# Stacking a short row chunk into 128 partitions with masked tables, and splitting more units of a fused Fourier and gated feed-forward kernel

## The chip, the cores and the metric

One NeuronCore of a Trainium2 chip runs the whole program. The metric is the device time of one execution in microseconds (us); medians are over the fast runs (granted TensorE clock 0.996 to 1.000). The engines are PE (TensorE, matmul), DVE (VectorE), ACT (ScalarE), POOL (GpSimd) and SP (which issues DMAs here).

## The reference

```
def reference(x, w_gate, w_val, w_out):          # x: 8 x 3008 x 256
    X = fft(fft(x, axis=1), axis=2).real         # Fourier mixing over rows and channels
    X = X.reshape(24064, 256)
    g = X @ w_gate                               # 256 -> 1536
    v = X @ w_val
    return (silu(g) * v) @ w_out                 # 1536 -> 256
```

## The kernel before

The row transform uses the symmetries of the Fourier sum. Each batch of 3008 rows is folded on POOL into cosine and sine coefficient rows: a chunk A of 128 rows and a short chunk C of 61 rows. Chunk C of two batches shares a 128-partition tile: the even batch has partitions 0 to 63, the odd one 64 to 127. PE multiplies the coefficients (weights) with tables `Tab` (moving side). A batch has two parts, each in two halves `eo`, each half with a `v` and a `g` product (`q`). The code is shortened:

```
def blocks(b, q):
    p0 = 64 * (b % 2)
    return [(0, slice(0, P), *coef_a(b)),                                 # chunk A: 128 rows
            (1, slice(p0, p0 + 64) if b else slice(0, P), *coef_c(b))]    # chunk C: 64 rows
...
for j, (ch, r, CE, BB) in enumerate(blk):
    for eo in eos:
        for kind in range(2):
            if part == 0:   # 189 or 188 columns, one block of columns for each kind
                cols = slice(0, GH + 1) if kind == 0 else slice(GH + 1, NCE)
                l, r_ = CE[r, q, eo, kind, 0:P], tab[:, eo, cols]
            else:           # 376 columns, both kinds added into the same ones
                l, r_ = BB[r, q, eo, kind, 0:P], tab[:, (eo + kind) % 2, NOO:NTAB]
            nc.tensor.matmul(ps[eo][:, cols], l, r_, ...)
if part == 0 and 1 in eos:
    row0(b, q, ps[1])       # weights of ONE column, result added to row 0 of ps[1]
# after each half: ACT copies v from PSUM (od), DVE adds and subtracts g and od into Pt, Qt
```

The transform of a batch is a job put between two "units" of the feed-forward part. A unit is one block of 128 hidden channels for one tile of up to 512 columns; there are 24 tiles of 12 units. A column pair (row k and row -k) shares the products with `Pt` and `Qt`. An unsplit unit takes 6 matmuls; a split one takes 5 and reconstructs the second value by an instruction on DVE and a multiplication on POOL:

```
SPLIT     = (0, 2, 3, 5, 6, 8, 9, 11)             # tiles 3 to 20
SPLIT_END = (0, 1, 2, 3, 5, 6, 7, 8, 9, 11)       # tiles 21, 22
def split(u):
    return 3 <= u[0] < nT - 1 and u[1] in (SPLIT if u[0] < t_end else SPLIT_END)

# part_a: g = Wp.Pt + Wq.Qt ; v = Wp.Pt
#   split:   ACT  sp = silu(g) ; DVE es = bc * w0 + v
#   unsplit: v += Wq.Qt ; ACT sg = silu(g) ; DVE hp = sg * v
# part_b (one unit later): g += Wm.Qt
#   split:   v += Wq.Qt ; DVE vv = 2 es - v ; ACT sgv = silu(g) ; POOL hm = sgv * vv ; DVE hp = sp * v
#   unsplit: v += Wm.Qt ; ACT sg = silu(g) ; DVE hm = sg * v
```

Between these, 8 output matmuls (`o<-Wo,hp` and `o<-Wo,hm`, 256 columns) of the tile before are put into each unit. The kernel uses eight banks of PSUM (the memory that matmuls write): three for `g`, three for `v`, two for the output.

Of the kernel before, what the change touches and what calls it, by code (L numbers as in the profile page):

```python
# [31 lines left out]
def kernel(  # L32
# [25 lines left out]
    t0 = [sum(wide[:t]) for t in range(nT)]  # L58


    NCE = 2 * GH + 1
    NOO = NCE + GH + 1
    NTAB = NOO + G
# [9 lines left out]

    const = ctx.enter_context(tc.tile_pool(name="const", bufs=1))
    cp = ctx.enter_context(tc.tile_pool(name="coef", bufs=2))
    pqp = ctx.enter_context(tc.tile_pool(name="pq", bufs=5))
    odp = ctx.enter_context(tc.tile_pool(name="od", bufs=2))
    psG = ctx.enter_context(tc.tile_pool(name="psG", bufs=3, space=bass.MemoryType.PSUM))
# [18 lines left out]
    sgn = const.tile([P, 1], F32, name="sgn")  # L97
    XA = const.tile([P, 8, 2, D], F32, name="XA")
    XC = const.tile([P, 8, 2, D], F32, name="XC")
    SDf = const.tile([P, 2, 4, D], F32, name="SDf")  # L100
    EOf = const.tile([P, 2, 4, P + 1], F32, name="EOf")
    Af = const.tile([P, 2, 2, P + 1], F32, name="Af")

# [42 lines left out]

    def fold_steps(eng, X, CE, BB, q, r):
        tt = eng.tensor_tensor
        F = SDf[r, q]
        E, O = EOf[r, 0], EOf[r, 1]  # L150
        up, down = X[r, 0:4, q], X[r, 7:3:-1, 1 - q]

        def cross():
            tt(F[:, :, 1:D], up[:, :, 1:D], down[:, :, D - 1:0:-1], op=Alu.add)
            tt(E[:, :, P:P + 1], up[:, :, 0:1], down[:, :, 0:1], op=Alu.add)

        def even():
            tt(E[:, :, 0:P], F[:, :, P:0:-1], F[:, :, P:D], op=Alu.add)

        def odd():  # L160
            tt(O[:, :, 0:P], F[:, :, P:0:-1], F[:, :, P:D], op=Alu.subtract)

        def ab():
            tt(Af[r], EOf[r, :, 0:2, :], EOf[r, :, 2:4, :], op=Alu.add)

        def ce():
            tt(CE[r, q, :, 0, :], Af[r, :, 0, :], Af[r, :, 1, :], op=Alu.add)
            tt(CE[r, q, :, 1, :], Af[r, :, 0, :], Af[r, :, 1, :], op=Alu.subtract)

        def bb():  # L170
            quarter_rows(tt, E, O, BB[r, q])

        return [cross, even, odd, ab, ce, bb]
# [3 lines left out]
        tt(B_[:, 1], O[:, 0:2, 0:P], O[:, 2:4, 0:P], op=Alu.subtract)  # L177
        tt(B_[:, 1, :, 0:1], E[:, 3::-3, P:P + 1], E[:, 1:3, P:P + 1], op=Alu.subtract)

    coefA, coefC = {}, {}  # L180

    def coef_a(b):
        if b not in coefA:
# [1 line left out]
                        cp.tile([P, 2, 2, 2, P], BF16, name="BBa"))  # L185
        return coefA[b]

    def coef_c(b):
        p = b if b < 2 else 1 + b // 2
        if p not in coefC:  # L190
            coefC[p] = (cp.tile([P, 2, 2, 2, P + 1], BF16, name="CEc"),
                        cp.tile([P, 2, 2, 2, P], BF16, name="BBc"))
        return coefC[p]



# [125 lines left out]
    def weigh(lo, hi):  # L322
        vts(Tab[:, 1, 1, :, lo:hi], Tab[:, 1, 1, :, lo:hi], scalar1=wC, scalar2=None, op0=Alu.mult)
# [8 lines left out]
            nc.gpsimd.dma_start(out=dst, in_=src.rearrange("(no p) f -> p no f", p=P)[:, :, fc * T:(fc + 1) * T])  # L332

    CEa, BBa = coef_a(0)
    CEc, BBc = coef_c(0)


    ti = [tp.tile([P, 2, NCE], I32, name=f"t1{ch}") for ch in range(2)]
# [63 lines left out]

    def heads(eng, ev, od, CE):

        eng.tensor_tensor(CE[:, :, 0, 0, P:P + 1], ev, od, op=Alu.add)
        eng.tensor_tensor(CE[:, :, 0, 1, P:P + 1], ev, od, op=Alu.subtract)

    acc = [[None, None], [None, None]]

# [128 lines left out]
    pl, ql = pq_tiles(nT - 1)  # L538
    last = (pl[:, w_last:w_last + B], ql[:, w_last:w_last + B])

    def blocks(b, q):

        p0 = 64 * (b % 2)
        return [(0, slice(0, P), *coef_a(b)), (1, slice(p0, p0 + 64) if b else slice(0, P), *coef_c(b))]

    def row0(b, q, ps):
        for ch, r, CE, BB in blocks(b, q):
            for kind, cols in ((0, slice(0, GH + 1)), (1, slice(GH + 1, NCE))):
                nc.tensor.matmul(ps[0:1, cols], CE[r, q, 0, kind, P:P + 1], Tab[r, ch, q, 0, cols],  # L549
                                 start=False, stop=True, skip_group_check=True)  # L550

    def transform(b, part, eos, given=None):
        n = NCE if part == 0 else G
        ev, ods = {}, {}
        for q, pool, nm in ((0, psV, "v"), (1, psG, "g")):
            if given:
                ps = {eo: given[eo][q] for eo in eos}
                blk = []
            else:
                ps = {eo: pool.tile([P, T], F32, name=nm) for eo in eos}  # L560
                blk = blocks(b, q)
            for j, (ch, r, CE, BB) in enumerate(blk):
                tab = Tab[r, ch, q]
                for eo in eos:
                    for kind in range(2):
                        if part == 0:
                            cols = slice(0, GH + 1) if kind == 0 else slice(GH + 1, NCE)
                            l, r_ = CE[r, q, eo, kind, 0:P], tab[:, eo, cols]
                        else:
                            cols = slice(0, G)  # L570
                            l = BB[r, q, eo, kind, 0:P]
                            r_ = tab[:, (eo + kind) % 2, NOO:NTAB]
                        nc.tensor.matmul(ps[eo][:, cols], l, r_, start=(j == 0 and kind == 0),  # L573
                                         stop=(j == len(blk) - 1 and kind == 1), skip_group_check=True)
            if part == 0 and 1 in eos and not given:

                row0(b, q, ps[1])
            for eo in eos:
                if q == 0:
                    ods[eo] = odp.tile([P, NCE], F32, name="od")  # L580
                    nc.scalar.copy(ods[eo][:, 0:n], ps[eo][:, 0:n])
                else:
                    ev[eo] = ps[eo]

        def put(eo, dst, s0, w, minus):
            nc.vector.tensor_tensor(dst, ev[eo][:, s0:s0 + w], ods[eo][:, s0:s0 + w],  # L586
                                    op=Alu.subtract if minus else Alu.add)

        if part == 0:
            runs = [(0, GH, 1, 0), (GH, GH, 0, 1), (G, GH, GH + 1, 0), (G + GH, GH, GH + 1, 1)]  # L590
        else:
            runs = [(2 * G, G, 0, 0), (3 * G, G, 0, 1)]
        todo = []
        for eo in eos:
            for c0, n_, s0, minus in runs:
                for t, off, src, w in pieces(b * H + c0, n_):
                    todo.append((t, eo, off, s0 + src, w, minus))
        for t, eo, off, s0, w, minus in sorted(todo, key=lambda v: v[0:2]):
            put(eo, pq_tiles(t)[eo][:, off:off + w], s0, w, minus)
        if part == 0:  # L600
            for eo in eos:
                put(eo, last[eo][:, b:b + 1], 0, 1, 0)
# [98 lines left out]
    state = {}  # L701
    owork = None

    SPLIT = (0, 2, 3, 5, 6, 8, 9, 11)
    SPLIT_END = (0, 1, 2, 3, 5, 6, 7, 8, 9, 11)
    t_end = tile_of((B - 1) * H) + 1

    bc = {}

    def split(u):  # L710

        return 3 <= u[0] < nT - 1 and u[1] in (SPLIT if u[0] < t_end else SPLIT_END)

    def part_a(u):
        t, f = u
# [31 lines left out]
    def part_b(u):  # L747
# [4 lines left out]
        fs = slice(f * P, (f + 1) * P)  # L752
        nc.tensor.matmul(g[:, :w], Wm[:, 0, fs], Qt[:, :w], start=False, stop=True, skip_group_check=True)  # L753
        if kept:
            nc.tensor.matmul(v[:, :w], Wq[:, 1, fs], Qt[:, :w], start=False, stop=True, skip_group_check=True)  # L755
            sp, es = kept
            vm = vvp.tile([P, T], F32, name="vv")
            nc.vector.scalar_tensor_tensor(vm[:, w - 1::-1], es[:, :w], 2.0, v[:, :w],  # L758
                                           op0=Alu.mult, op1=Alu.subtract)
            sm = sgv.tile([P, T], F32, name="sgv")  # L760
            nc.scalar.activation(sm[:, w - 1::-1], g[:, :w], AF.Silu)  # L761
            nc.gpsimd.tensor_tensor(hts[t][1][:, f, :w], sm[:, :w], vm[:, :w], op=Alu.mult)  # L762
            nc.vector.tensor_tensor(hts[t][0][:, f, :w], sp[:, :w], v[:, :w], op=Alu.mult)  # L763
            return
        nc.tensor.matmul(v[:, :w], Wm[:, 1, fs], Qt[:, :w], start=False, stop=True, skip_group_check=True)  # L765
        sg = sgp.tile([P, T], F32, name="sg")
# [21 lines left out]
        lo += 1  # L788
    queue = {}
    act_at = {}  # L790

    def run_loads(n):
        for _, fn in loads[:n]:
# [3 lines left out]
    def fold_step(what, i, unit):  # L797
# [4 lines left out]
        if j == 0:  # L802
            if kind == "A":
                queue[what] = fold_steps(nc.gpsimd, XA, *coef_a(b), q, slice(0, P))
            else:
                queue[what] = fold_steps(nc.gpsimd, XC, *coef_c(b), q, slice(64 if b == 1 else 0, P))
        queue[what].pop(0)()
        if q == 1 and j == 0:
            act_at.setdefault(max(unit + 2, 11), []).append(what)

    def load_next(what):
        kind, b = what
# [22 lines left out]
    def weight_unit(fc, gv):  # L835
        return [lambda k=k: weights(fc, gv, k) for k in range(2)]

    raO = SDf.rearrange("p k a d -> p (k a d)")[:, 0:4 * G].rearrange("p (c q n) -> p c q n", c=2, q=2)

    def angles_o(ch):  # L840
        return [lambda: angles(rrO[:, ch], kfO, ch, rrO[:, ch].bitcast(I32)),
# [5 lines left out]
    def sine_o(ch):  # L847
# [2 lines left out]
    before = {0: angles_o(0), 1: weight_unit(1, 0), 2: weight_unit(1, 1), 3: angles_o(1) + cosine_o(0),  # L850
              4: weight_unit(2, 0) + cosine_o(1), 5: weight_unit(2, 1), 7: sine_o(0), 8: sine_o(1),
              9: [lambda: weigh(NOO, NTAB), lambda: value_rows((1, 2))]}
    loads = []

    prev = None
    owork = None
    for i, u in enumerate(units):
        t, f = u
        if f == 0 and split((t, SPLIT[0])):
            ps = psG.tile([P, T], F32, name="g")  # L860
            w = width(t)
            nc.tensor.matmul(ps[:, :w], sel, pq_tiles(t)[1][:, :w], start=True, stop=True)  # L862
            bc.pop(t - 2, None)
            bc[t] = bcp.tile([P, T], F32, name="bc")
            nc.scalar.copy(bc[t][:, :w], ps[:, :w])
        for fn in before.pop(i, ()):
            fn()
# [14 lines left out]
            fold_step(what, j, i)  # L882
        for what in act_at.pop(i, ()):
            load_next(what)
        if i in job_at:
            whole_part(*job_at[i])
        prev = u
# [35 lines left out]
```

## Time and profile before

| reading | value |
|---|---|
| time, median (range) of 3 runs | 673.16 us (672.6 to 673.18) |
| PE / DVE / ACT / POOL busy | 98 / 82 / 65 / 63% of 670.8 us |
| chain that ended last | PE 94% |
| split units | 164 of 288 |
| length of a middle tile: no transform / with a part 0 / with a part 1 | 24.51 / 27.76 / 27.89 us |

A tile's length is the distance between the starts of its first `g` matmul and of the next tile's, read from the timeline. The head of the program is the part up to the first unit, mostly input DMAs.

The first lines of the profile of the kernel before (engine, busy us, share, instructions; PEld are PE's weight loads; then the chain of waits, by engine):

```profile
PE 656.5 (98%) x4269; PEld 411.6 (61%) x4336; DVE 549.4 (82%) x957; ACT 433.5 (65%) x764; POOL 423.8 (63%) x455
...
PE 94%; DVE 2%; DMA 2%; issue 1%; POOL 1%; ACT 0%; DVEq 0%; ACTq 0%; POOLq 0%
```

PE's 98% alone would prove little. The Trainium skill says so too ("Perfetto Trace Analysis", Identifying the Most-Contended Engine: matmul busy time is a bad measure, because matmuls are pipelined), and this case agrees: its profiles read 98, 97 and 98% for kernels of 671, 651 and 634 us. What counts is the distance between starts. In the timeline a 512-column matmul recorded as 0.38 us is followed by the next after 0.216 us. Apart from single steps of 0.43 us (a matmul whose record is missing), PE has no holes in units.

DVE must be read in the same way. The timeline of DVE in tile 22 of the kernel before, which already had 10 split units (start us, duration us, instruction):

```profile
628.75 0.74 DVE L735 SCALAR_TENSOR_TENSOR es<-bc,w,v 128x512 f32<-128x512 f32 x1
629.50 0.69 DVE L758 SCALAR_TENSOR_TENSOR vv<-es,v 128x512 f32<-128x512 f32 x1
630.11 0.68 DVE L763 TENSOR_TENSOR hp<-sp,v 128x512 bf16<-128x512 f32 x1
630.70 0.74 DVE L735 SCALAR_TENSOR_TENSOR es<-bc,w,v 128x512 f32<-128x512 f32 x1
```

The three durations add up to 2.11 us, yet the next round starts after 1.95 us: two of the three records run about 0.08 us into the next one. The 1.95 us are also PE's period (5 x 0.216 + 8 x 0.109), and two other rounds of this kernel are shorter (1.85 and 1.86 us). So DVE is led by PE here, although it looks full; e8 and e9 test it.

The timeline of PE in a part 0 of the kernel before (x2 merges two matmuls):

```profile
383.94 0.33 PE L573 MATMUL v<-Tab,CEa 128*128 128x189 bf16 x2
384.21 0.34 PE L573 MATMUL v<-Tab,CEc 64*128 64x189 bf16 x2
384.48 0.34 PE L573 MATMUL g<-Tab,CEa 128*128 128x189 bf16 x2
384.75 0.33 PE L573 MATMUL g<-Tab,CEc 64*128 64x189 bf16 x2
385.11 0.33 PE L573 MATMUL v<-Tab,CEa 128*128 128x189 bf16 x2
385.36 0.34 PE L573 MATMUL v<-Tab,CEc 64*128 64x189 bf16 x2
385.63 0.33 PE L549 MATMUL v<-Tab,CEa 128*1 128x189 bf16 x2
```

Two matmuls of 189 and 188 columns take 0.162 us at the pace of 81 ns that they have within a pair where no change of rows comes before it, but the pairs start 0.27 us apart. Each change between 128 and 64 rows costs some 0.1 us. The groups of weight loads tell the same as idle time of "issue" (columns: count | busy us, mean ns | idle us before):

```profile
L573 PEld LDWEIGHTS <-BBa 128*128 128x128 bf16 x64 | 4.5, 97 | 7.8 <-issue 7.2
...
L573 PEld LDWEIGHTS <-CEa 128*128 128x128 bf16 x56 | 4.3, 97 | 3.6 <-issue 3.2 <-POOL BBa L176 0.2
...
L573 PEld LDWEIGHTS <-CEc 64*128 64x128 bf16 x56 | 3.1, 95 | 4.4 <-issue 4.4
L573 PEld LDWEIGHTS <-BBc 64*128 64x128 bf16 x56 | 3.1, 94 | 8.7 <-issue 8.7
```

### The profile page before, as it was taken

To read this page: it belongs to the slowest core of one execution; us is meant where nothing else is said; L and a number is where in the kernel's file an instruction comes from. 1 tells how busy PE (TensorE), PEld (TensorE's weight loads), DVE (VectorE), ACT (ScalarE), POOL (GpSimd) and SP (SyncE) were. 2 spreads that over 40 slices of the span, in tenths; PEclk is the share of its full clock that TensorE was granted. 3 is DMA by queue.
4 is the path that set the end of the run, shared out by engine and by line. 5 is a ranking of instruction groups with operands and counts; after the bars stand their busy time and mean duration, and the time that the engine had idled before them with its cause. 6 is when DMAs were issued, how large, how long until landed. Compare 5 with 4: busy or idle time off the path is not lost.

```text
span 670.8 us, 12888 instructions
## 1 busy us (share of the span) xinstructions
PE 656.5 (98%) x4269; PEld 411.6 (61%) x4336; DVE 549.4 (82%) x957; ACT 433.5 (65%) x764; POOL 423.8 (63%) x455
## 2 busy tenths in 40 slices
PE   8889999999999999999999999999999999999997
PEld 5446666666656666565665666655665656656676
DVE  8796667888888888888888888888888888889962
ACT  8576566666566576575665666656666657666663
POOL 8895953687676787776675767667576333435510
PEclk9999999999999999999999999999999999999999
DMA  9856355335215213344143111125111011111112
GB/s 217 121 76 124 111 127 136 89 92 143 61 33 136 69 50 107 90 98 104 36 109 97 48 33 48 40 68 129 48 41 41 33 44 36 48 32 48 48 48 72
DMA packets 45564, 52.53 MB, mean 78 GB/s; under 512 B 6290, under 2 KB 33466, under 8 KB 45498
## 3 DMA queue, kind: packets, MB, share of 16 engines
q1 hardware_dynamic: 42314, 49.35, 28.0%
q0 software_dynamic: 3184, 2.36, 3.0%
q8 instruction: 34, 0.56, 0.4%
q14 instruction: 32, 0.26, 0.1%
HBM read 29.39 MB, written 24.65 MB: 81 GB/s over the span
## 4 chain that ended last, share of the span: by engine, by line
PE 94%; DVE 2%; DMA 2%; issue 1%; POOL 1%; ACT 0%; DVEq 0%; ACTq 0%; POOLq 0%
PE o L683 37%; PE g L723 16%; PE v L723 14%; PE g L753 9%; PE v L755 5%; PE v L765 4%; PE g L573 3%; PE v L573 3%; DMA W<-in_moe_w_val_dram 2%; PE g L862 1%; PE v L549 1%; PE g L549 1%; PE o L434 1%; DVE hp L744 0%; DVE hm L768 0%
## 5 line engine op out<-in xcount | busy, mean ns | idle before, releaser
L762 POOL TENSOR_TENSOR hm<-sgv,vv 128x512 bf16<-128x512 f32 (+1 forms) x164 | 208.3, 1271 | 190.2 <-DVE vv L758 180.9
L683 PE MATMUL o<-Wo,hp 128*128 128x256 bf16 (+2 forms) x1140 | 169.7, 273 | 0.0
L683 PE MATMUL o<-Wo,hm 128*128 128x256 bf16 (+2 forms) x1140 | 169.7, 273 | 0.0
L683 PEld LDWEIGHTS <-hp 128*128 128x128 bf16 (+2 forms) x1140 | 112.2, 99 | 69.3
L683 PEld LDWEIGHTS <-hm 128*128 128x128 bf16 (+2 forms) x1140 | 112.0, 98 | 69.2 <-issue 0.2
L733 ACT ACTIVATE sp<-g 128x512 f32<-128x512 f32 (+1 forms) x164 | 98.0, 597 | 73.6 <-PE g L723 48.6
L735 DVE SCALAR_TENSOR_TENSOR es<-bc,w,v 128x512 f32<-128x512 f32 (+1 forms) x164 | 121.8, 743 | 5.9 <-PE v L723 5.1
L758 DVE SCALAR_TENSOR_TENSOR vv<-es,v 128x512 f32<-128x512 f32 (+1 forms) x164 | 112.6, 686 | 13.7 <-PE v L755 10.3
L761 ACT ACTIVATE sgv<-g 128x512 f32<-128x512 f32 (+1 forms) x164 | 98.2, 599 | 39.1 <-PE g L753 39.1
L768 DVE TENSOR_TENSOR hm<-sg,v 128x512 bf16<-128x512 f32 (+2 forms) x124 | 82.3, 663 | 41.7 <-ACT sg L767 32.3
L763 DVE TENSOR_TENSOR hp<-sp,v 128x512 bf16<-128x512 f32 (+1 forms) x164 | 111.3, 679 | 0.0
L723 PE MATMUL v<-Pt,Wp 128*128 128x512 bf16 (+2 forms) x288 | 107.9, 375 | 3.4
L723 PE MATMUL g<-Pt,Wp 128*128 128x512 bf16 (+2 forms) x288 | 108.0, 375 | 0.0
L753 PE MATMUL g<-Qt,Wm 128*128 128x512 bf16 (+2 forms) x288 | 107.9, 375 | 0.0
L744 DVE TENSOR_TENSOR hp<-sg,v 128x512 bf16<-128x512 f32 (+2 forms) x124 | 82.4, 664 | 26.6 <-ACT sg L743 24.8
L743 ACT ACTIVATE sg<-g 128x512 f32<-128x512 f32 (+2 forms) x124 | 71.9, 580 | 36.1 <-PE g L723 26.9
L767 ACT ACTIVATE sg<-g 128x512 f32<-128x512 f32 (+2 forms) x124 | 71.9, 580 | 32.5 <-PE g L753 32.3
L723 PE MATMUL g<-Qt,Wq 128*128 128x512 bf16 (+2 forms) x223 | 83.3, 373 | 0.5 <-DVE Qt L586 0.5
L723 PEld LDWEIGHTS <-Wp 128*128 128x128 bf16 x576 | 56.3, 98 | 40.9 <-issue 4.2
L755 PE MATMUL v<-Qt,Wq 128*128 128x512 bf16 (+1 forms) x164 | 62.1, 378 | 0.0
L689 ACT COPY ev<-o 128x512 f32<-128x512 f32 x90 | 52.8, 587 | 7.9 <-PE o L683 7.0
L723 PEld LDWEIGHTS <-Wq 128*128 128x128 bf16 x412 | 40.3, 98 | 19.9 <-issue 0.3
(165 smaller groups left out, 631.2 us busy)
## 6 DMA issues: line engine op xcount, KB each, us to landing
out_dram<-ev SPq DMA_DIRECT2D x96, 128.0 KB
XA<-in_x_dram SPq DMA_DIRECT2D x32, 256.0 KB
XA<-in_x_dram SPq DMA_DIRECT2D x112, 64.0 KB
XC<-in_x_dram SPq DMA_DIRECT2D x32, 120.0 KB
XC<-in_x_dram SPq DMA_DIRECT2D x105, 32.0 KB
out_dram<-ev SPq DMA_DIRECT2D x12, 120.0 KB
out_dram<-ev SPq DMA_DIRECT2D x10, 112.0 KB
XA<-in_x_dram SPq DMA_DIRECT2D x1, 1024.0 KB
```

Source lines behind the costliest of these rows:

```text
L683: nc.tensor.matmul(ps[:n, j, :], hts[minus][:, f, c:c + n], Wo[:, f, :], start=(f == 0), stop=(f == nF - 1))
L723: nc.tensor.matmul(ps[:, :w], Wt[:, gv, fs], src[:, :w], start=start, stop=stop, skip_group_check=True)
L733: nc.scalar.activation(sg[:, :w], g[:, :w], AF.Silu)
L735: nc.vector.scalar_tensor_tensor(es[:, :w], bc[t][:, :w], w0[:, f:f + 1], v[:, :w], op0=Alu.mult, op1=Alu.add)
L744: nc.vector.tensor_tensor(hts[t][0][:, f, :w], sg[:, :w], v[:, :w], op=Alu.mult)
L753: nc.tensor.matmul(g[:, :w], Wm[:, 0, fs], Qt[:, :w], start=False, stop=True, skip_group_check=True)
L755: nc.tensor.matmul(v[:, :w], Wq[:, 1, fs], Qt[:, :w], start=False, stop=True, skip_group_check=True)
L758: nc.vector.scalar_tensor_tensor(vm[:, w - 1::-1], es[:, :w], 2.0, v[:, :w], op0=Alu.mult, op1=Alu.subtract)
L761: nc.scalar.activation(sm[:, w - 1::-1], g[:, :w], AF.Silu)
L762: nc.gpsimd.tensor_tensor(hts[t][1][:, f, :w], sm[:, :w], vm[:, :w], op=Alu.mult)
L763: nc.vector.tensor_tensor(hts[t][0][:, f, :w], sp[:, :w], v[:, :w], op=Alu.mult)
L768: nc.vector.tensor_tensor(hts[t][1][:, f, w - 1::-1], sg[:, :w], v[:, :w], op=Alu.mult)
```

## The change

The intent is to take matmul work off PE in two ways. First, for batches 1 to 7 the two kinds of chunk C are stacked: kind 0 in partitions 0 to 63 and kind 1 in 64 to 127 of a tile `St`. POOL folds into `Fc`, and two DMAs per batch move it. The tables of chunk C are masked with zeros (part 0), or copied with one half reversed (part 1), so that one 128-row matmul does the work of two 64-row ones. Second, more units are split. Cut to its core:

```diff
+    def spread_c(b, F):
+        for half, b_ in ((0, b), (1, b + 1)) if b > 1 else ((1, b),):
+            for kind in range(2):
+                nc.sync.dma_start(out=stack(b_)[64 * kind:64 * kind + 64, :], in_=F[64 * half:64 * half + 64, kind])
...
+    def products(b, part, q, eo):
+        CE, BB = coef_a(b)
+        if part == 0:
+            return ([(CE[:, q, eo, k, 0:P], Tab[:, 0, q, eo, e], e) for k, e in ((0, E0), (1, E1))] +
+                    [(stack_of(b, 0)[:, q, eo, 0:P], Tab[:, 1, q, eo, 0:NCE], slice(0, NCE))])
+        res = [(BB[:, q, eo, k, 0:P], Tab[:, 0, q, (eo + k) % 2, NOO:NTAB], slice(0, G)) for k in range(2)]
+        if b:
+            return res + [(stack_of(b, 1)[:, q, eo, :], Tab[:, 0:2, q, eo, NCE:NCE + GH], slice(0, G))]
... (batch 0 keeps its two products; row0 likewise takes one stacked product instead of two)
-    SPLIT = (0, 2, 3, 5, 6, 8, 9, 11)
-    SPLIT_END = (0, 1, 2, 3, 5, 6, 7, 8, 9, 11)
+    SPLIT = (0, 1, 2, 3, 5, 6, 7, 8, 9, 11)
+    SPLIT_END = (0, 1, 2, 3, 4, 6, 7, 8, 9, 10, 11)
-        return 3 <= u[0] < nT - 1 and u[1] in (SPLIT if u[0] < t_end else SPLIT_END)
+        return 3 <= u[0] and u[1] in (SPLIT if u[0] < t_end else SPLIT_END)
...
+    def halve_tables():
+        nc.gpsimd.memset(Tab[0:64, 1, :, :, GH + 1:NCE], 0.0)
+        nc.gpsimd.memset(Tab[64:P, 1, :, :, 0:GH + 1], 0.0)
... (odd_table: four DVE copies for part 1; the broadcast bc is kept in bf16; eight more columns in the last tile's hp)
```

More of the change, by code (lines that the diff above doesn't have):

```diff
@@ L58 @@
     t0 = [sum(wide[:t]) for t in range(nT)]
+    R2 = 4 * G
     NCE = 2 * GH + 1
@@ L75 @@
     cp = ctx.enter_context(tc.tile_pool(name="coef", bufs=2))
+    fcp = ctx.enter_context(tc.tile_pool(name="fc", bufs=1))
+    stp = ctx.enter_context(tc.tile_pool(name="st", bufs=3))
     pqp = ctx.enter_context(tc.tile_pool(name="pq", bufs=5))
@@ L99 @@
     XC = const.tile([P, 8, 2, D], F32, name="XC")
-    SDf = const.tile([P, 2, 4, D], F32, name="SDf")
+    SDf = const.tile([P, R2 // D + 1, D], F32, name="SDf")
     EOf = const.tile([P, 2, 4, P + 1], F32, name="EOf")
@@ L148, in fold_steps @@
         tt = eng.tensor_tensor
-        F = SDf[r, q]
+        F = SDf[r, 0:4]
         E, O = EOf[r, 0], EOf[r, 1]
@@ L178, in quarter_rows @@
         tt(B_[:, 1, :, 0:1], E[:, 3::-3, P:P + 1], E[:, 1:3, P:P + 1], op=Alu.subtract)
-    coefA, coefC = {}, {}
+    coefA, stacks = {}, {}
+    NE = P + 1
+    ND = NE + P
     def coef_a(b):
@@ L186, in coef_a, with stack, stack_of @@
         return coefA[b]
-    def coef_c(b):
-        p = b if b < 2 else 1 + b // 2
-        if p not in coefC:
-            coefC[p] = (cp.tile([P, 2, 2, 2, P + 1], BF16, name="CEc"),
-                        cp.tile([P, 2, 2, 2, P], BF16, name="BBc"))
-        return coefC[p]
+    def stack(b):
+        if b not in stacks:
+            stacks[b] = stp.tile([P, 4 * ND], BF16, name="St")
+        return stacks[b]
+    def stack_of(b, part):
+        S4 = stack(b).rearrange("p (q e n) -> p q e n", q=2, e=2)
+        return S4[:, :, :, 0:NE] if part == 0 else S4[:, :, :, NE:ND]
+    def spread_c(b, F):
+        for half, b_ in ((0, b), (1, b + 1)) if b > 1 else ((1, b),):
+            for kind in range(2):
+                nc.sync.dma_start(out=stack(b_)[64 * kind:64 * kind + 64, :], in_=F[64 * half:64 * half + 64, kind])
     tmp_ctx = ExitStack()
@@ L334 @@
     CEa, BBa = coef_a(0)
-    CEc, BBc = coef_c(0)
+    CEc = tp.tile([P, 2, 1, 2, 1], BF16, name="CEc")
+    BBc = stack(0)[:, 0:8 * P].rearrange("p (q e k d) -> p q e k d", q=2, e=2, k=2)
     ti = [tp.tile([P, 2, NCE], I32, name=f"t1{ch}") for ch in range(2)]
@@ L403, in heads @@
     def heads(eng, ev, od, CE):
-        eng.tensor_tensor(CE[:, :, 0, 0, P:P + 1], ev, od, op=Alu.add)
-        eng.tensor_tensor(CE[:, :, 0, 1, P:P + 1], ev, od, op=Alu.subtract)
+        eng.tensor_tensor(CE[:, :, 0, 0, -1:], ev, od, op=Alu.add)
+        eng.tensor_tensor(CE[:, :, 0, 1, -1:], ev, od, op=Alu.subtract)
     acc = [[None, None], [None, None]]
@@ L539 @@
     last = (pl[:, w_last:w_last + B], ql[:, w_last:w_last + B])
-    def blocks(b, q):
-        p0 = 64 * (b % 2)
-        return [(0, slice(0, P), *coef_a(b)), (1, slice(p0, p0 + 64) if b else slice(0, P), *coef_c(b))]
+    E0, E1 = slice(0, GH + 1), slice(GH + 1, NCE)
     def row0(b, q, ps):
-        for ch, r, CE, BB in blocks(b, q):
-            for kind, cols in ((0, slice(0, GH + 1)), (1, slice(GH + 1, NCE))):
-                nc.tensor.matmul(ps[0:1, cols], CE[r, q, 0, kind, P:P + 1], Tab[r, ch, q, 0, cols],
-                                 start=False, stop=True, skip_group_check=True)
+        CE = coef_a(b)[0]
+        todo = [(CE[:, q, 0, k, P:P + 1], Tab[:, 0, q, 0, e], e) for k, e in ((0, E0), (1, E1))]
+        if b:
+            todo.append((stack_of(b, 0)[:, q, 0, P:P + 1], Tab[:, 1, q, 0, 0:NCE], slice(0, NCE)))
+        else:
+            todo += [(CEc[:, q, 0, k, 0:1], Tab[:, 1, q, 0, e], e) for k, e in ((0, E0), (1, E1))]
+        for l, r_, cols in todo:
+            nc.tensor.matmul(ps[0:1, cols], l, r_, start=False, stop=True, skip_group_check=True)
+    def products(b, part, q, eo):
[4 more added lines that the diff above has]
+        res = [(BB[:, q, eo, k, 0:P], Tab[:, 0, q, (eo + k) % 2, NOO:NTAB], slice(0, G)) for k in range(2)]
+        if b:
+            return res + [(stack_of(b, 1)[:, q, eo, :], Tab[:, 0:2, q, eo, NCE:NCE + GH], slice(0, G))]
+        return res + [(BBc[:, q, eo, k, :], Tab[:, 1, q, (eo + k) % 2, NOO:NTAB], slice(0, G)) for k in range(2)]
     def transform(b, part, eos, given=None):
@@ L557, in transform @@
                 ps = {eo: given[eo][q] for eo in eos}
-                blk = []
             else:
                 ps = {eo: pool.tile([P, T], F32, name=nm) for eo in eos}
-                blk = blocks(b, q)
-            for j, (ch, r, CE, BB) in enumerate(blk):
-                tab = Tab[r, ch, q]
                 for eo in eos:
-                    for kind in range(2):
-                        if part == 0:
-                            cols = slice(0, GH + 1) if kind == 0 else slice(GH + 1, NCE)
-                            l, r_ = CE[r, q, eo, kind, 0:P], tab[:, eo, cols]
-                        else:
-                            cols = slice(0, G)
-                            l = BB[r, q, eo, kind, 0:P]
-                            r_ = tab[:, (eo + kind) % 2, NOO:NTAB]
-                        nc.tensor.matmul(ps[eo][:, cols], l, r_, start=(j == 0 and kind == 0),
-                                         stop=(j == len(blk) - 1 and kind == 1), skip_group_check=True)
+                    mms = products(b, part, q, eo)
+                    for i, (l, r_, cols) in enumerate(mms):
+                        nc.tensor.matmul(ps[eo][:, cols], l, r_, start=(i == 0), stop=(i == len(mms) - 1),
+                                         skip_group_check=True)
             if part == 0 and 1 in eos and not given:
@@ L754, in part_b @@
         if kept:
-            nc.tensor.matmul(v[:, :w], Wq[:, 1, fs], Qt[:, :w], start=False, stop=True, skip_group_check=True)
+            wp = w + (B if t == nT - 1 else 0)
+            nc.tensor.matmul(v[:, :wp], Wq[:, 1, fs], Qt[:, :wp], start=False, stop=True, skip_group_check=True)
             sp, es = kept
@@ L762, in part_b @@
             nc.gpsimd.tensor_tensor(hts[t][1][:, f, :w], sm[:, :w], vm[:, :w], op=Alu.mult)
-            nc.vector.tensor_tensor(hts[t][0][:, f, :w], sp[:, :w], v[:, :w], op=Alu.mult)
+            nc.vector.tensor_tensor(hts[t][0][:, f, :wp], sp[:, :wp], v[:, :wp], op=Alu.mult)
             return
@@ L790 @@
     act_at = {}
+    spread_at = {}
+    foldC = {}
     def run_loads(n):
@@ L805, in fold_step @@
             else:
-                queue[what] = fold_steps(nc.gpsimd, XC, *coef_c(b), q, slice(64 if b == 1 else 0, P))
+                if q == 0:
+                    foldC[b] = fcp.tile([P, 2, 4 * ND], BF16, name="Fc")
+                F5 = foldC[b].rearrange("p k (q e n) -> p q e k n", q=2, e=2)
+                queue[what] = fold_steps(nc.gpsimd, XC, F5[..., 0:NE], F5[..., NE:ND], q,
+                                         slice(64 if b == 1 else 0, P))
         queue[what].pop(0)()
@@ L809, in fold_step @@
             act_at.setdefault(max(unit + 2, 11), []).append(what)
+        if kind == "C" and q == 1 and j == 5:
+            spread_at[unit + 2] = b
     def load_next(what):
@@ L836, in weight_unit @@
         return [lambda k=k: weights(fc, gv, k) for k in range(2)]
-    raO = SDf.rearrange("p k a d -> p (k a d)")[:, 0:4 * G].rearrange("p (c q n) -> p c q n", c=2, q=2)
+    raO = SDf.rearrange("p a d -> p (a d)")[:, 0:4 * G].rearrange("p (c q n) -> p c q n", c=2, q=2)
     def angles_o(ch):
@@ L852, with odd_table @@
               9: [lambda: weigh(NOO, NTAB), lambda: value_rows((1, 2))]}
+    def halve_tables():
+        nc.gpsimd.memset(Tab[0:64, 1, :, :, GH + 1:NCE], 0.0)
+        nc.gpsimd.memset(Tab[64:P, 1, :, :, 0:GH + 1], 0.0)
+    def odd_table(c, half):
+        r = slice(64 * half, 64 * half + 64)
+        src = Tab[r, 1, :, :, NOO + GH * c:NOO + GH * (c + 1)]
+        nc.vector.tensor_copy(Tab[r, c, :, :, NCE:NCE + GH], src[:, :, ::-1] if half else src)
+    before[17] = before.get(17, []) + [halve_tables]
+    for i in range(4):
+        before[13 + i] = [lambda i=i: odd_table(i // 2, i % 2)]
     loads = []
@@ L860 @@
             ps = psG.tile([P, T], F32, name="g")
-            w = width(t)
+            w = width(t) + (B if t == nT - 1 else 0)
             nc.tensor.matmul(ps[:, :w], sel, pq_tiles(t)[1][:, :w], start=True, stop=True)
             bc.pop(t - 2, None)
-            bc[t] = bcp.tile([P, T], F32, name="bc")
+            bc[t] = bcp.tile([P, T], BF16, name="bc")
             nc.scalar.copy(bc[t][:, :w], ps[:, :w])
@@ L884 @@
             load_next(what)
+        if i in spread_at:
+            spread_c(spread_at[i], foldC[spread_at[i]])
         if i in job_at:
```

## The prediction

> **What bounds it now.** PE does. The page has PE busy 656.5 of 670.8 us (98%), and the chain of waits is 94% PE. Because matmul durations overlap, I used the distance between starts in the timeline: a 512-column matmul follows the previous one after 0.216 us, a 256-column one after 0.109, a 376-column one after 0.159. Those spacings add up to nearly the whole span from 50 us on; the holes that remain are missing records of one matmul each, the stalls below, and the head. DVE reads 82%, but its records overlap too: an instruction recorded at 0.68 us is followed by the next after 0.60.
>
> **What the change takes off PE.**
> 1. Split units have 5 matmuls instead of 6. They go from 164 (the count of the es group) to 213: 38 more of 512 columns (0.216 us) and 11 in the last tile of 320 (about 0.136). That is 9.7 us, less 0.1 for one more broadcast: 9.6.
> 2. In part 1 of each transform from batch 1 on, the two 64-row matmuls become one 128-row matmul: 4 x 0.159 us x 7 batches = 4.5. Part 0 keeps its columns (189+188 become 377) and saves only instructions.
> 3. Stalls at 128-row/64-row switches. In a transform's timeline every change between 128x128 and 64x128 costs 0.09 to 0.10 us, with the weight load exposed: 12 per batch in part 0, 8 in part 1. The Trainium skill, "TensorEngine Tiling (Array Packing)", Key Properties, says that a change of tiling mode drains the array; this trace agrees, at 0.095. Afterwards the rows are always 128. The one-column matmuls of row 0 still switch (batch 0 shows 0.09 into and 0.10 out of a 128x1 run), 4 times a batch. 16 x 0.095 x 7 = 10.6.
> Sum 24.7 us.
>
> **What it adds.** A split unit costs DVE about 1.87 us back to back, against 1.95 us of PE (5 x 0.216 + 8 x 0.109), and POOL 1.23. Tile 22, already at 10 of 12, kept full PE pace with DVE reading 100%. So PE should stay the bound, with DVE thin behind it. POOL, with folds, gets near 90% in the fold stretches; three buffers absorb that. DVE table copies, POOL memsets and stack DMAs fall in slack.
>
> **What is lost again.** In part 0 the second half needs the v bank that the previous unit's hp frees, about 1.16 us after the transform starts; the trace already shows 0.09 us of waiting there. The quicker first half (0.65 us, before 1.07) will wait about 0.5, in part 1 about 0.2. Over 7 batches that gives back some 4 us. So about 21 of 25 us arrive; the critical path is PE throughout.
>
> **Predicted:** 673.2 - 21 = 652 us, range 646.5 to 658.5. Faster by over 2%: 0.91; within 2%: 0.08; slower: 0.01.
>
> **Signs.** PE matmuls 118 fewer, less missing records (49 for splits, +1 broadcast, 70 in transforms); no 64-row groups from batch 1 on; transform starts without the 0.095 steps except around row 0; a new wait of PE v of the transform on DVE hp, 0.2 to 0.5 us each; a middle tile without transform 24.5 -> 24.1 us; DVE near 88%, POOL near 75%, PE still 97% or more.
>
> **What would make it wrong.** DVE or POOL becoming the bound in runs of five split units (PE waiting on hp, DVE on hm; tiles then 24.5 us or more, time near 660); PE waiting for the stack DMA; a longer tail because the last unit's hm now goes through POOL; or no bank wait, giving 648.

## The result, and the profile after

The changed kernel took 652.75 us (652.49 to 652.97, 4 runs) against 673.07 us (4 runs) of the kernel before; the ratio is 0.9699, 95% interval 0.9683 to 0.9716. Ratios here are the mean time of one kernel's fast runs over that of the other's of the same rounds, so not quite the ratio of the medians quoted. The prediction said 652.0, range 646.5 to 658.5.

The same first lines of the profile of the changed kernel:

```profile
PE 633.5 (97%) x4151; PEld 407.3 (63%) x4218; DVE 573.9 (88%) x1010; ACT 433.8 (67%) x765; POOL 481.1 (74%) x506
...
PE 93%; DVE 3%; issue 1%; POOL 1%; ACT 1%; DVEq 0%; ACTq 0%; POOLq 0%
```

PE has 118 matmul records fewer (4269 to 4151), as counted in advance, and is still the chain. DVE and POOL rose to 88 and 74%, as said.

PE's timeline in the same part 0 of the changed kernel (the bracket is idle time and what ended it):

```profile
372.91 0.33 PE L587 MATMUL v<-Tab,CEa 128*128 128x189 bf16 x2
373.07 0.32 PE L587 MATMUL v<-Tab,St 128*128 128x377 bf16 x1
373.23 0.33 PE L587 MATMUL g<-Tab,CEa 128*128 128x189 bf16 x2
373.40 0.32 PE L587 MATMUL g<-Tab,St 128*128 128x377 bf16 x1
373.96 0.33 PE L587 MATMUL v<-Tab,CEa 128*128 128x189 bf16 x2 [0.24 <-ACT od L595]
374.12 0.32 PE L587 MATMUL v<-Tab,St 128*128 128x377 bf16 x1
374.38 0.33 PE L564 MATMUL v<-Tab,CEa 128*1 128x189 bf16 x2
374.54 0.32 PE L564 MATMUL v<-Tab,St 128*1 128x377 bf16 x1
374.79 0.34 PE L587 MATMUL g<-Tab,CEa 128*128 128x189 bf16 x2
```

The steps from A to C are now 0.16 to 0.17 us: no stall. Around the one-column weights of row 0 the steps of 0.25 us (0.16 of work and 0.09) remain. And there is the predicted wait: from 373.40, where the work would allow the next matmul at 373.56, to 373.96. PE lost 0.40 us there, and about as much in each of the 7 batches. The profile names ACT's copy `od` as the releaser. Here are the two candidates in the timeline:

```profile
373.35 0.68 DVE L778 TENSOR_TENSOR hp<-sp,v 128x512 bf16<-128x512 f32 x1
...
373.43 0.48 ACT L595 COPY od<-v 128x377 f32<-128x377 f32 x1 [0.32 <-PE v L587]
```

`hp` is recorded until 374.03, after the waiting matmul has started; `od` until 373.91, 0.05 us before it. So in part 0 the second half took the bank of the first half's `v`, not that of the previous unit, and my prediction named the wrong releaser there. The two ended nearly together, so it is luck that the size came out close. (In the built program that matmul waits on a semaphore of ScalarE alone, in all seven batches.)

In part 1 it is otherwise. The same place in a part 1 of the changed kernel:

```profile
424.25 0.68 DVE L778 TENSOR_TENSOR hp<-sp,v 128x512 bf16<-128x512 f32 x1
...
424.49 0.47 ACT L595 COPY od<-v 128x376 f32<-128x376 f32 x1 [0.47 <-PE v L587]
424.61 0.33 PE L587 MATMUL g<-Tab,St 128*128 128x376 bf16 x1
...
424.99 0.48 PE L587 MATMUL v<-Tab,BBa 128*128 128x376 bf16 x2
```

The second half starts 0.38 us after the last product of the first, of which 0.159 are work: a wait of 0.22 us. Both candidates have ended by then (`hp` at 424.93, `od` at 424.96), but in the built program this matmul waits on a semaphore of VectorE alone, and its `v` has the bank of the previous unit's `v`. So the releaser is `hp`, as predicted, in part 1 of batches 2 to 7; in batch 1 it is `od` again.

The weight loads of chunk C no longer wait for "issue" (2.2 us of idle time before 64 loads, against 4.4 and 8.7 before 56 each; those of chunk A still do, above all at the bank waits):

```profile
L587 PEld LDWEIGHTS <-St 128*128 128x128 bf16 x64 | 6.3, 98 | 2.2
```

Lengths of tiles in us from the traces; each run's tiles of a kind agree to within 0.02 us unless a range is given:

| kernel | no transform | with part 0 | with part 1 | last tile and end | whole, without head |
|---|---|---|---|---|---|
| before | 24.51 | 27.76 | 27.89 | 33.13 | 644.8 |
| changed | 24.08 | 26.82 | 26.43 | 32.21 | 625.2 |
| e1, stack alone | 24.51 | 27.25 | 26.86 | 33.65 | 634.5 |
| e2, split alone | 24.08 | 27.33 | 27.46 | 31.66 | 635.4 |
| e3, columns back | 24.08 | 26.82 | 26.75 | 32.21 | 627.4 |
| e4, switches back | 24.08 | 27.48 | 26.88 | 32.19 | 632.9 |
| e5, halves in two units | 24.08 | 26.43 | 26.00 | 32.20 | 619.3 |
| e6, row 0 wide | 24.08 | 26.51 | 26.43 | 32.20 | 622.9 |
| e8, 11 of 12 split | 23.90 | 26.64 | 26.25 | 32.20 | 622.0 |
| e9, 12 of 12 split | 23.68 | 26.43 to 26.56 | 26.03 | 32.19 | 618.5 |
| e12, e5 and e6 | 24.08 | 26.03 | 26.00 | 32.20 | 616.5 |
| e13, e12 and all split | 23.68 | 25.63 to 25.73 | 25.60 | 32.07 | 609.1 |

(The middle tiles 7 to 20 are shown; "whole" is the span less the head.) From before to changed, a tile without a transform gains 0.43 us, exactly two matmuls of 0.216. A tile with part 0 gains another 0.51 and one with part 1 another 1.03.

### The profile page after: what moved, and what is told of

It is laid out like the page before. It is cut to its first block, busy times and chain, and to the rows that moved or that the text cites. A ratio compares the mean times of both kernels' runs of the same rounds, so it can differ in the third digit from the quotient of the medians.

```text
span 650.8 us, 12791 instructions
## 1 busy us (share of the span) xinstructions
PE 633.5 (97%) x4151; PEld 407.3 (63%) x4218; DVE 573.9 (88%) x1010; ACT 433.8 (67%) x765; POOL 481.1 (74%) x506
## 4 chain that ended last, share of the span: by engine, by line
PE 93%; DVE 3%; issue 1%; POOL 1%; ACT 1%; DVEq 0%; ACTq 0%; POOLq 0%
PE o L697 38%; PE g L737 17%; PE v L737 13%; PE g L767 9%; PE v L770 7%; PE v L780 2%; PE v L587 2%; PE g L587 1%; DVE Pt L600 1%; PE g L898 1%; PE g L438 1%; ACT od L595 1%; PE v L438 1%; PE v L564 1%; DVE hp L758 0%
## 5 line engine op out<-in xcount | busy, mean ns | idle before, releaser
L777 POOL TENSOR_TENSOR hm<-sgv,vv 128x512 bf16<-128x512 f32 (+2 forms) x213 | 265.6, 1252 | 133.1 <-DVE vv L773 122.7
L747 ACT ACTIVATE sp<-g 128x512 f32<-128x512 f32 (+2 forms) x213 | 125.5, 589 | 80.2 <-PE g L737 51.8
L749 DVE SCALAR_TENSOR_TENSOR es<-bc,w,v 128x512 f32<-128x512 bf16 (+2 forms) x213 | 155.8, 731 | 5.3 <-PE v L737 5.1
L776 ACT ACTIVATE sgv<-g 128x512 f32<-128x512 f32 (+2 forms) x213 | 125.7, 590 | 47.7 <-PE g L767 46.7
L773 DVE SCALAR_TENSOR_TENSOR vv<-es,v 128x512 f32<-128x512 f32 (+2 forms) x213 | 143.9, 676 | 11.5 <-PE v L770 3.8
L778 DVE TENSOR_TENSOR hp<-sp,v 128x512 bf16<-128x512 f32 (+2 forms) x213 | 142.6, 669 | 0.0
L770 PE MATMUL v<-Qt,Wq 128*128 128x512 bf16 (+2 forms) x213 | 79.9, 375 | 0.0
L783 DVE TENSOR_TENSOR hm<-sg,v 128x512 bf16<-128x512 f32 (+2 forms) x75 | 50.8, 678 | 23.8 <-ACT sg L782 16.3
L758 DVE TENSOR_TENSOR hp<-sg,v 128x512 bf16<-128x512 f32 (+2 forms) x75 | 50.8, 678 | 13.2 <-ACT sg L757 7.4
L757 ACT ACTIVATE sg<-g 128x512 f32<-128x512 f32 (+2 forms) x75 | 44.3, 591 | 21.0 <-PE g L737 16.1
L782 ACT ACTIVATE sg<-g 128x512 f32<-128x512 f32 (+2 forms) x75 | 44.4, 592 | 17.7 <-PE g L767 17.1
```

What stands on the lines that cost most here:

```text
L747: nc.scalar.activation(sg[:, :w], g[:, :w], AF.Silu)
L749: nc.vector.scalar_tensor_tensor(es[:, :w], bc[t][:, :w], w0[:, f:f + 1], v[:, :w], op0=Alu.mult, op1=Alu.add)
L758: nc.vector.tensor_tensor(hts[t][0][:, f, :w], sg[:, :w], v[:, :w], op=Alu.mult)
L770: nc.tensor.matmul(v[:, :wp], Wq[:, 1, fs], Qt[:, :wp], start=False, stop=True, skip_group_check=True)
L773: nc.vector.scalar_tensor_tensor(vm[:, w - 1::-1], es[:, :w], 2.0, v[:, :w], op0=Alu.mult, op1=Alu.subtract)
L776: nc.scalar.activation(sm[:, w - 1::-1], g[:, :w], AF.Silu)
```

## The experiments

Theory: PE is the bound throughout, so the gain is a sum of PE terms: matmuls of split units, columns of part 1, and drains at changes of the array's tiling mode; less the waits for PSUM banks in the transforms. Rivals: VectorE is the bound, or becomes it; the two parts of the change need each other; the steps of 0.095 us are no mode switches. All runs gave the right result, and each was timed beside the kernel before (medians there 672.65, 671.97 and 672.39 us).

### e1: the stack alone

```diff
-    SPLIT = (0, 1, 2, 3, 5, 6, 7, 8, 9, 11)
-    SPLIT_END = (0, 1, 2, 3, 4, 6, 7, 8, 9, 10, 11)
+    SPLIT = (0, 2, 3, 5, 6, 8, 9, 11)
+    SPLIT_END = (0, 1, 2, 3, 5, 6, 7, 8, 9, 11)
-        return 3 <= u[0] and u[1] in ...
+        return 3 <= u[0] < nT - 1 and u[1] in ...
```

> The stack with its masked tables alone; the split units are those of the kernel before (8 of 12, 10 at the end, none in the last tile). If PE bounds everywhere and the two parts add, only the transform tiles gain: by the tile lengths of the two traces 0.51 us in each tile with a part 0 and 1.04 in each with a part 1, 7 of each, so about 10.9 us: 662.2 us. The rival, that DVE is the bound of the kernel before and the gain comes from somewhere else than PE, expects little here (DVE work is unchanged): above 668.

Measured 662.25 us (661.46 to 662.88), ratio 0.9847 (0.9834 to 0.9861). Tiles without a transform are as before, those with one gain 0.51 and 1.03 us. DVE work per unit did not change, and yet the time fell by 10 us: PE was the bound. The end of the program is 0.52 us longer, after the last matmul, which still ends 29.43 us into the last tile as before. This comes with the stack (e2, without it, has 3.69 us there, the kernel before 3.70, e1 4.22); what in it takes the time is not shown.

### e2: the split alone

The kernel before, with the changed kernel's SPLIT, SPLIT_END and condition, its bf16 broadcast, and its eight more columns in the last tile.

> The split units of the changed kernel (10 of 12, 11 at the end, last tile, broadcast kept in bf16) with the old 64-row transforms. If PE bounds and the parts add: 0.43 us per middle tile and 0.9 at the end, about 8.8 us: 664.3 us. The rival, that the added DVE and POOL work of the split needs the room that the stack made, expects clearly less than half of that: above 668.5, with tiles that hold a transform longer than 27.4 us.

Measured 662.76 us (662.13 to 663.82), ratio 0.9857 (0.9844 to 0.9871). The parts are independent: without the head, 10.28 us (e1) and 9.35 us (e2) add up to 19.63, and both together gave 19.61. The split does not need the stack's room on any engine.

### e3: the removed columns of part 1 given back

```diff
+    zw = const.tile([P, P], BF16, name="zw")
+    nc.vector.memset(zw, 0.0)
...
-            return res + [(stack_of(b, 1)[:, q, eo, :], ...
+            return res + [(zw, Tab[:, 1, q, eo, NOO:NTAB], slice(0, G)),
+                          (stack_of(b, 1)[:, q, eo, :], ...
```

> The changed kernel with the 376 columns given back to each part 1 group, as a product with zero weights (128 rows, so no switch of mode; the result is the same): 28 x 0.159 = 4.5 us more PE work. By plain sums of PE work it costs 4.5 us: 657.2. If part 1 also waits for PSUM banks (0.22 us before its second half, 0.22 before the next unit), part of the columns hides in these waits: about 0.3 us for each batch, 2 us: 654.8.

Measured 654.56 us (654.18 to 655.88), ratio 0.9736 (0.9723 to 0.9749). A tile with part 1 grew by 0.32 us, where 4 x 0.159 = 0.64 us of matmul were added: the other half vanished in waits. So of the 4.5 us that the prediction books for these columns only 7 x 0.32 = 2.2 us reach the clock. The stack's matmul saving is the smaller part of its gain.

### e4: the switches of rows given back

```diff
+        sw = [(stack_of(b, 1)[0:64, q, eo, :], Tab[0:64, 1, q, eo, GH + 1:GH + 9], slice(0, 8))]
... (`sw` goes before the stacked product in both parts; the table there is zero)
```

> The changed kernel with one 64-row product of zeros by 8 columns put before each stack product: 8 per batch, each with a switch to 64 rows and back, and nearly no columns. It gives back the 16 switches per batch that the prediction counted. If each drains the array for 0.095 us: 0.215 us per insertion; those of the first half of a transform partly hide behind the wait for the ScalarE copy of v, so about 1.07 us per batch, 7.5 us: 660.2. With nothing hidden 12 us: 664.7. If the 0.095 us steps had another cause than the switch of rows (the rival: the weights' new source tile), about 0.03 us per insertion, 1.5 us in all: 654.2.

Measured 659.99 us (659.96 to 661.68), ratio 0.9821 (0.9807 to 0.9834). Tiles grew by 0.66 us (part 0) and 0.45 (part 1), 1.11 per batch against 1.07 expected. PE's timeline in a part 1 of e4 (x2 is the product of 8 columns and the stacked one behind it):

```profile
428.14 0.48 PE L588 MATMUL v<-Tab,BBa 128*128 128x376 bf16 x2
428.56 0.45 PE L588 MATMUL v<-Tab,St 64*128 64x8 bf16 x2
428.84 0.48 PE L588 MATMUL g<-Tab,BBa 128*128 128x376 bf16 x2
```

Two products of 376 columns need 0.318 us, but 0.42 pass to the 64-row one: a product with 8 columns costs a stall of about 0.1 us on each side, which I take for the drain of the array. A cause in the weights' source tile is out, since `St` as 128-row weights shows no such step in the changed kernel. This run also settles the releaser in part 0: the two switches in the first `v` put its end, and with it the copy `od`, 0.22 us later, and the second half starts 1.27 us after the transform's start instead of 1.05. `hp`, which the inserted products do not touch, is recorded to the same 1.13 us in both.

Another rival is that a product this short cannot hide the weight load of the next one. I ran no short product of 128 rows as a control, but the head of the same trace has some: eight products of ONE column with 128-row weights, each with its own load of 0.10 us, start 0.025 us apart (0.20 us for all eight), so shortness alone does not cost 0.1 us.

```profile
24.72 0.34 PE L468 MATMUL o<-SDt,W 128*128 128x1 bf16 x8
24.92 0.36 PE L738 MATMUL g<-Pt,Wp 128*128 128x480 bf16 x1
```

### e5: the halves of a transform in consecutive units

```diff
         if i in job_at:
-            whole_part(*job_at[i])
+            transform(*job_at[i], (0,))
+        if i - 1 in job_at:
+            transform(*job_at[i - 1], (1,))
```

> The changed kernel with the second half of each transform moved one unit later, so that the two halves never follow each other. Theory: the PE waits inside and behind the transforms (0.40 us in part 0, 0.22 + 0.22 us in part 1, 7 batches, 5.9 us) are waits for PSUM banks that ScalarE and VectorE still read, and a unit of matmuls between the halves hides them: tiles with part 0 from 26.82 to about 26.4 us, with part 1 from 26.43 to 26.0; 646.9 us. Rival: DVE is by now the bound (it reads 100% in these tiles), and moving work cannot help: 652 us or more.

Measured 647.50 us (646.13 to 647.71), ratio 0.9628 (0.9614 to 0.9643). The tiles fell by 0.40 and 0.43 us, the full size of the waits, without one instruction less. DVE is not the bound, and the lost part of the prediction was a matter of PSUM banks. Part 1's 0.43 us are two waits of 0.22: one inside it (shown above), and one behind it that I had not predicted. The second, between the stacked product at 425.79 and the next unit's `g`, in the timeline of the changed kernel:

```profile
425.79 0.32 PE L587 MATMUL g<-Tab,St 128*128 128x376 bf16 x1
...
426.16 0.38 PE L737 MATMUL g<-Pt,Wp 128*128 128x512 bf16 x1
```

A product of 376 columns is followed after 0.159 us when nothing is in the way, here after 0.375. The last of DVE's additions from the first half's `g` (`Pt<-g,od`) ends at 426.11 in that timeline, 0.05 us before the matmul. In the trace the matmul waits on DVE's semaphore alone. That it is this addition that frees the bank is read from the order in time; no run took DVE's additions alone out of the way.

### e6: the weights of row 0 widened to 128 columns

```diff
+    R0 = const.tile([P, 2, 3, P], BF16, name="R0")          # zeros but for column 0
+            nc.scalar.copy(R0[:, :, 0:2, 0], coef_a(b)[0][:, :, 0, :, P])
+            nc.scalar.copy(R0[:, :, 2, 0], stack_of(b, 0)[:, :, 0, P])
... (row0, for b > 0)
-            nc.tensor.matmul(ps[0:1, cols], l, r_, ...)
+            nc.tensor.matmul(ps[:, cols], R0[:, q, j, :], r_, ...)
```

> The changed kernel with the one-column weights of row 0 padded to 128 columns of zeros (same columns streamed, two small ScalarE copies per batch). If the 0.09 us before and after each row 0 group is a switch of the array's column mode, 4 per batch go away: 0.38 us, 2.7 us in all, less what the small copies delay: 650.0 to 651.5. If it were the change of source tile or the PSUM row, nothing: 652.7.

Measured 651.60 us (650.66 to 651.64), ratio 0.9689 (0.9673 to 0.9705), just above the 650.0 to 651.5 expected. Its interval overlaps that of the changed kernel (0.9683 to 0.9716), so the times alone prove nothing; the traces do: every tile with a part 0 is 0.31 to 0.37 us shorter, and no other tile moved. Of 4 x 0.095 = 0.38 us most arrives. So a change from 128 weight columns to one and back also costs about 0.09 us each time, and wider weights of zeros are cheaper than narrow ones here. (The built programs agree that the mode changes: these products have the tile size 128x32 in the changed kernel and 128x128 in e6.)

### e8 and e9: 11 and 12 of 12 units split

```diff
-    SPLIT = (0, 1, 2, 3, 5, 6, 7, 8, 9, 11)
+    SPLIT = (0, 1, 2, 3, 5, 6, 7, 8, 9, 10, 11)      # e8;  tuple(range(12)) in e9
```

> The changed kernel with unit 10 of the middle tiles split too (11 of 12). PE work falls by 0.216 us in each of 18 tiles, 3.9 us. If PE is still the bound and DVE keeps up (1.87 us a split unit against 1.95 of PE): about 649 us, middle tile without transform 24.08 to 23.87. If DVE is the bound at 10 of 12 already: no gain or a loss, 652.5 us or more, with PE waiting for DVE.

> The changed kernel with all units of the middle tiles split. PE work falls by 0.43 us in each of 18 tiles, 7.8 us: 645 us if PE stays the bound. DVE then has 12 x 1.87 = 22.4 us and some 1.5 us of transform work per tile of about 25: no unsplit unit is left in which it catches up after a transform, so I expect part of it to be lost, some 647 to 651; if DVE is the bound by then, a middle tile without transform is no shorter than 23.9 us.

Measured 650.02 us (649.22 to 650.81), ratio 0.9670 (0.9655 to 0.9685), and 646.89 us (646.86 to 647.48), ratio 0.9625 (0.9611 to 0.9640). e9 came out just below the 647 to 651 that I expected. The eleventh split unit takes 0.18 us off a tile without a transform and the twelfth all of the 0.216 that each could give. VectorE was not the bound at 10 of 12, and hardly at 12; only in some tiles with a part 0 was 0.13 us of e9's gain lost. The missing 0.04 us per tile are a step of 0.256 us, where 0.216 would do, behind the broadcast matmul at each tile's start, in e8 as in e9. In both traces the matmul behind it waits on ScalarE's semaphore, and a `sgv` ends 0.05 us before it.

### e12 and e13: together

> The halves in two units and the wide row 0 weights together, split units as in the changed kernel. With the bank waits gone the row 0 saving is no longer cut short by the next wait: 5.8 us + 7 x 0.38 us = 8.5 us, 644 us; if they overlap, 646.

e12 (e5 and e6) measured 643.76 us (643.35 to 644.90), ratio 0.9579 (0.9563 to 0.9595). The tiles with part 0 fall by 0.79 us, 0.40 and 0.39: with the banks out of the way the row 0 saving arrives in full.

> The same with every unit of tiles 3 to 23 split. By PE work 0.43 us less in each of 18 tiles and 0.2 in the last three, 8.2 us: 636 us. Measured before, 12 of 12 gave 0.39 of the 0.43 in most tiles: 637 us. If DVE becomes the bound now that PE needs under 25.5 us for a tile with a transform, its lag shows as PE waiting in the tiles with a part 0: 639 to 641.

e13 also splits all units of tiles 3 to 23 (SPLIT and SPLIT_END are `tuple(range(12))`). It measured 636.72 us (636.28 to 637.25), ratio 0.9470 (0.9456 to 0.9484): the best version here, 16 us under the changed kernel. Its page says that PE is still the chain. The first fence has the same lines of its page as before; the second has the busy times in the stretch of 300 to 560 us (length, then PE, PEld, DVE, ACT, POOL) and shows how full VectorE reads:

```profile
PE 623.8 (98%) x4179; PEld 406.5 (64%) x4179; DVE 588.6 (93%) x1049; ACT 434.9 (69%) x779; POOL 528.2 (83%) x546
...
PE 96%; DVE 2%; POOL 1%; issue 0%; ACT 0%; DVEq 0%; ACTq 0%; POOLq 0%
```

```profile
300.00:560.00 260.00, 260.00 (x1738) 169.14 (x1736) 256.83 (x439) 182.20 (x323) 220.83 (x205) 1.00 0.22 62
```

DVE is recorded busy for 256.83 of 260 us, and still PE waits almost nowhere: from tile 4 to 22 its longest wait is 0.10 us, in three tiles with a part 0.

## Why the prediction was right

- **The bound.** Right. PE is the chain before and after, and e1, e5 and e9 each moved the time by PE terms alone, with DVE unchanged or busier.
- **Split, 9.6 us.** Right: 9.35 us in e2, and the trace gives 0.43 us for each of the middle tiles. Where it was off is the end: tile 22 did not get shorter (+0.04), for its extra split unit (-0.216) is eaten by the last tile's new broadcast (0.14, which I had booked) and a wait of 0.12 us behind it, which I had not (the next matmul waits for ScalarE, as in e8).
- **The stack, 15.1 less 4 us.** The net of 11.1 was near the 10.3 of e1, and the single terms are now measured: returning 16 switches per batch costs 7 x 1.11 = 7.8 us (e4, which includes the own time of the 56 products put in), returning the columns 2.2 us (e3). Both are below the booked 10.6 and 4.5, because a part of each would have been spent waiting. These two returns sum to 10.0 us.
- **The mode switches.** Right in kind and size: 0.094 to 0.106 us a switch in e4's trace, and 0.09 for the one-column weights, confirmed by e6. The Trainium skill ("TensorEngine Tiling (Array Packing)", Key Properties) says only that changing the mode drains the array. The number came from the trace.
- **The bank wait.** The size was near: 0.40 us in part 0 (I said 0.5) and 0.22 in part 1 (I said 0.2). The step that failed is its cause in part 0, "the v bank that the previous unit's hp frees": there it was the copy `od` of the first half, as the profile's releaser, the program's semaphore and e4 show. That `od` and `hp` end within 0.13 us of each other there is luck. In part 1 the cause was right but for batch 1: the program waits for DVE, and `hp` ends 0.05 us before the second half starts. I also missed the second wait of 0.22 us behind part 1, for the `g` bank. It makes the loss 7 x (0.40 + 0.43) = 5.8 us gross, or, less the 0.09 us per part 0 that the kernel before already waited, 5.2 where I had said "some 4".
- **The engines behind.** Right: DVE 88 and POOL 74% against "near 88" and "near 75". The fear that runs of five split units would make them the bound did not come true; nor does it at twelve.
- **The end.** A longer tail from POOL's last product did not show: the last matmul ends 27.97 us into the last tile instead of 29.43, the 1.5 us of the split. What follows the last matmul took back 0.5.

## What to carry to other kernels

Judge a pipelined engine by the distance between starts, not by its busy share: in e13 DVE's records fill 99% of a stretch while PE still sets the pace, with four DVE instructions more in each middle tile than in the kernel before. Keep all weights of a stretch at one array shape (pad rows and columns with zeros if need be), because each change of shape cost about 0.095 us here, more than a 188-column product (0.081). When a job between two steady stages gets shorter, look for who still reads its PSUM banks: the saving stops there, and moving half of the job one unit later gave back all of it (5.8 us by tile lengths) with no instruction added.

## What the Trainium skill lacked or had wrong

- "TensorEngine Tiling (Array Packing)", Key Properties, says that a change of tiling mode drains the array, but gives no size: 0.094 to 0.106 us at each change between 128x128 and 64x128 (e4), and about 0.09 between 128 weight columns and one (e6). That page does not say that single-column weights among full ones pay this (the built program gives them the tile size 128x32).
- "TensorE: Matmul & The Clock Gate", Part 3, The mechanism, says that LDWEIGHTS overlaps with in-flight matmuls "only when row_grp differs" (the lines above it there also allow the background weight buffer). The runs show otherwise for weights over all 128 rows: loads of 98 ns are hidden behind matmuls of the same rows (512 columns every 0.216 us, 188 columns every 0.081), and a load is exposed where the number of rows or of weight columns changes.
- "Perfetto Trace Analysis", Identifying the Most-Contended Engine, takes the occupancy of the vector engine as a fair measure of how close it is to its limit. Here three recorded durations of 2.11 us repeat every 1.95 us, the shortest full rounds of these three start 1.85 us apart, and a stretch with DVE at 256.83 of 260 us is paced by PE.
